# Normalising the first block by subtract and multiply, and forming its first weights' low parts on GpSimd

## Chip, cores and metric

The kernel runs on one core of one Trainium2 chip. The metric is the device time of one execution in microseconds (us). Each time stands for one execution of the whole program.

## The reference

The kernel computes one transformer-like block on an input of 2048 rows and 448 columns, all in 32-bit floats. Cut to what matters:

```python
mod = (silu(c) @ w_mod).reshape(1, 6, 1, 448)
sa, ca, ga, sb, cb, gb = (mod[:, i] for i in range(6))
h = layernorm(x) * (1 + ca) + sa
x = x + ga * A(h, k, v, ...)      # short causal convolution, times v, long causal convolution, times h
h = layernorm(x) * (1 + cb) + sb
g, u = h @ w_gate, h @ w_up       # 448 x 1792 each
x = x + gb * ((sigmoid(g) * u) @ w_down)
```

The change lies at the seam of the two halves: the second layer norm of the first 512 rows, and the first products of `h` with `w_gate` and `w_up`.

## The kernel before

**Tiles.** The 2048 rows stand as 16 tiles of 128 rows in one tensor `x1`. Four tiles make a block of 512 rows. The first half (convolutions by a fast transform, the gate) is followed by the gated feed-forward part, which runs over pairs (a slice `q` of 256 columns of the weights, a pair of row blocks `n`).

**Precision.** Every product of the feed-forward part is made of three products in a reduced format (`fp32r`): a number is kept as a high part (a copy rounded to `fp32r`, made by an ACT copy) and a low part (the number less its high part, a subtraction with two inputs). `plain_hi` (L553) and `plain_lo` (L557) do this for a slice of weights of 128 x 512, `x_hi` and `x_lo` (L697, L702 to L705) for the rows. High times high, low times high and high times low are added up in PSUM.

**Order of the work.** Nothing is reordered: each engine works through its own queue in the order in which the program names the operations. In the first half that order is the string `ORDER`, written out by hand. An item names a function and its arguments. Those that matter here, all near the end of the string:

- `gb.0` (L383): GpSimd adds a gated part to rows of `x1`.
- `fh` (`first_forms`): starts a weight load and makes the high parts of four weight tiles of the first slice on ACT (L553).
- `gm.0.3` (L487, L488), `ga.3` and `ga.2` (L421): GpSimd instructions, each of 128 x 896 with two inputs. Their results are first needed far later, at the gate of the second and third tile groups of the left half.
- `st`, `gma`, `gaa`, `bs`, `bt` (L349, L399, L404, L407 to L411): DVE's last work of the first half, which ends in the mean and variance `mv` of the four tiles of block 0.
- `y` (L364): products on TensorE that give the output of the long convolution. After the string follow two more groups of them, for `y1[1]` and `y1[2]`.

**The opening** of the second half comes next, in this order:

1. `ln2_end(0, 0)`: ACT takes the square root (L506), DVE the reciprocal `rstd2` (L508) and, by an operation of 128 x 4 with two inputs, `nmr2` = -mean * `rstd2` (L509).
2. `norm_rows(0)`: the rows are normalised as `x1 * rstd2 + nmr2` into `xn`, rows 0 to 2 on DVE (L666), row 3 on ACT (L668). Columns 128 to 191 are wanted twice side by side, in `xd`; four ACT activations make that straight from `x1` (L841). Between the two ACT copies `y1[1]` (`y_copy`, L372).
3. TensorE turns `xn` in 128 x 128 pieces (`turn_one`, L848). The 448 columns are cut into four tiles t = 0 to 3; tile 1 reads `xd`, the others `xn`. Tiles 0 and 2 come first, a row at a time (rows 0, 3, 1, 2), then 3, then 1.
4. Scale and shift by `cols`: DVE makes the high parts of tiles 0 and 2 from PSUM (`norm_hi`, L844), ACT those of tiles 3 and 1 (`norm_full`, L691). Then ACT copies `y1[2]` and makes the full values of tiles 0, 1 and 3, and DVE the four low parts of the weights (L557).
5. `plain_half(0, 0, 0, 0)`: 22 products of TensorE (L894) for the first 128 columns, eleven steps of two, in the order `LATE`. A step (t, s, b, k) takes weight tile t, s = 0 high and s = 1 low, and the rows' form b (0 is `B11`, 1 is `B21`) at place k. Places 0 and 1 of a form are high parts, the others low parts; place 1 of `B11` holds a high part in its upper 64 partitions and a low part in its lower 64. After the 8th product `last_vector` makes the full value of tile 2 on ACT and the three subtractions that give the rows' low parts on DVE (L702, L703, L705). After the 16th product `last_block` puts 16 products of `y` (L364, for `y1[3]`) into TensorE's queue and the gate and normalisation of block 1 into those of DVE (L935, L383, L500, L557, L666) and ACT.

The load of the next raw weights (`load_gu(1, ...)`) waits on SyncE's queue until the low parts are made, since it overwrites the raw weights.

Of the kernel before, what the change touches and what calls it, by code (L numbers as in the profile page):

```python
# [12 lines left out]
AF = mybir.ActivationFunctionType  # L13
OP = mybir.AluOpType
# [3 lines left out]
P = 128  # L18
# [29 lines left out]
gn.0.3 s2v.1.2:2 le.2 tv.1.5 kx.1.4:0 sa.1.1:1 yc.1 tv.1.3 gn.0.2 gn.1.2 sa.1.0:3 tv.1.6 st.1.1 gm.1.3 sum.3 st.1.0 s2v.1.3:1 sc.3 m0.1.2:0 y.0.0:0  # L48
m1.1.2:2 m0.1.3:3 kx.1.5:1 sa.1.2:2 ga.1 yc.0 m1.1.3:1 s2v.1.4:0 st.1.2 ga.0 kx.1.6:2 sa.1.3:1 m0.1.4:0 m1.1.4:2 gm.1.2 part.5:2 st.1.3 s2v.1.5:3
kx.1.7:0 pc.5 sa.1.4:0 m0.1.5:3 m1.1.5:1 s2v.1.6:1 st.1.4 gb.1 sa.1.5:3 m0.1.6:0 s2v.1.7:0 gm.0.2 m1.1.6:2 sum.5 st.1.5 sa.1.6:1 sc.5 m0.1.7:3  # L50
m1.1.7:1 y10.0:2 gb.0 st.1.6 fh sa.1.7:0 gma.0 gaa.0 gm.0.3 y.0.3:1 st.1.7 bs.1 y10.1:0 yc.3 bs.3 bs.2 y.0.2:2 gma.1 gaa.1 bt.3 bt.2 ga.3 bt.1 yc.2
bs.0 bt.0 ga.2
"""

# [58 lines left out]
def adaln_conv_glu_kernel(ctx: ExitStack, tc: tile.TileContext, q, kT, v, ssm, consts, dskip,  # L113
                          wgu, wd, wmod, c1t, wbt, out):
    nc = tc.nc
    PE, ACT, DVE, POOL = nc.tensor, nc.scalar, nc.vector, nc.gpsimd
# [51 lines left out]
    x1 = px.tile([P, NG, D], F32, name="x1")  # L168
# [28 lines left out]
    eps = cols[:, 20:21]  # L197
# [7 lines left out]
    rstd2, nmr2 = rstd, nmr  # L205
    mv = small([P, NG, nc.vector.BN_AGGR_DIM], "mv")
# [163 lines left out]
    def y_copy(h, i, y):  # L370
        t = copy_home((i - 1) % 2 if h else i)
        ACT.activation(t, y, AF.Copy)  # L372
        return t
# [129 lines left out]
    def ln2_end(i0, n_act=2):  # L503
        for i, j, w in ((i0, i0 + n_act, 1.0 / D), (i0 + n_act, i0 + 4, 1.0)):
            if i < j:
                ACT.activation(rstd2[:, i:j], mv[:, i:j, 1], AF.Sqrt, bias=eps, scale=w)  # L506
        s = slice(i0, i0 + 4)
        DVE.reciprocal(rstd2[:, s], rstd2[:, s])  # L508
        DVE.scalar_tensor_tensor(nmr2[:, s], mv[:, s, 0], -1.0, rstd2[:, s], op0=OP.mult, op1=OP.mult)  # L509
# [45 lines left out]
    def plain_lo(q, t, eng=DVE):  # L555
        x = plain(q, t)
        eng.tensor_sub(x[:, 1], ring["raw"][:, t], x[:, 0])  # L557
# [27 lines left out]
        for t in (2, 0, 1, 3):  # L585
            plain_hi(0, t)

    DO["fh"] = first_forms
    homes = {}

    def run(order):
# [40 lines left out]
    late["g02"], late["g03"] = copy_home(2), copy_home(3)  # L632
    yc = []
    y1 = [None, stage_out(1, 1, "t")]
    ln2_end(0, 0)
    y1.append(stage_out(1, 2, "t"))
    pz_.close()
    pa_.close()
# [5 lines left out]
    xn = xs[:, :4 * D].rearrange("p (a c) -> p a c", c=D)  # L644
    xd = xs[:, 4 * D:].rearrange("p (a c) -> p a c", c=P)
    ts = xs[:, :2048].rearrange("p (k t c) -> p k t c", k=2, t=2)
    full = pn.tile([P, 9, 512], F32, name="full")
# [9 lines left out]
    st = [st_t[:, 2 * k:2 * k + 2] for k in range(3)]  # L657
    xf = {"B11": a0[:, 0:3], "B21": a0[:, 3:7], "B22": a0[:, 7:11], "B12": a0[:, 11:14]}
# [3 lines left out]
    def norm_rows(n, rows_=range(4)):  # L662
        for i in rows_:
            g = slice(4 * n + i, 4 * n + i + 1)
            if n == 0 and i < 3 or n == 1 and i % 2:
                DVE.tensor_scalar(xn[:, i], x1[:, 4 * n + i], rstd2[:, g], nmr2[:, g], op0=OP.mult, op1=OP.add)  # L666
            else:
                ACT.activation(xn[:, i], x1[:, 4 * n + i], AF.Identity, bias=nmr2[:, g], scale=rstd2[:, g])  # L668

    def dup(eng):  # L670
        o, x = xd.rearrange("p a (r c) -> p a r c", r=2), xn[:, :, P:P + 64].unsqueeze(2).to_broadcast([P, 4, 2, 64])
        if eng is ACT:
            ACT.activation(o, x, AF.Copy)
        else:
            eng.tensor_copy(o, x)
# [13 lines left out]
    def norm_full(n, t, y, out=None):  # L689
        o = full[:, 4 * (n % 2) + t] if out is None else out  # L690
        ACT.activation(o, y, AF.Identity, bias=cols[:, 5 + t:6 + t], scale=cols[:, t:t + 1])  # L691
        if out is None and n % 2 and t == 3:
            for r in (0, 64):
                nc.sync.dma_start(full[r:r + 64, 8], full[0:64, 7])
# [4 lines left out]
    def x_lo(name, eng=DVE):  # L699
        o, x = xf[name], x_src[name]  # L700
        if o.shape[1] == 3:
            eng.tensor_sub(o[64:128, 1], x[64:128, 1], o[64:128, 1])  # L702
            eng.tensor_sub(o[:, 2], x[:, 0], o[:, 0])  # L703
        else:
            eng.tensor_sub(o[:, 2:4], x, o[:, 0:2])  # L705
# [128 lines left out]
        for t in ts_:  # L834
            plain_lo(q, t)

    norm_rows(0)
    yc.append(y_copy(1, 1, y1[1]))
    for i in range(4):
        x = x1[:, i, P:P + 64].unsqueeze(1).to_broadcast([P, 2, 64])  # L840
        ACT.activation(xd[:, i].rearrange("p (r c) -> p r c", r=2), x, AF.Identity, bias=nmr2[:, i:i + 1], scale=rstd2[:, i:i + 1])  # L841

    def norm_hi(t, y, out):
        DVE.tensor_scalar(out, y, cols[:, t:t + 1], cols[:, 5 + t:6 + t], op0=OP.mult, op1=OP.add)  # L844

    def turn_one(t, pt, i):
        at, w = AT[t]
        PE.transpose(pt[:, i * P:(i + 1) * P], xn[:, i, at:at + w] if w == P else xd[:, i], ident)  # L848

    p02 = two("y", "pt_02")  # L850
    p0, p2 = p02[:, 0], p02[:, 1]
    p13 = two("t", "pt_13")
    for i in (0, 3, 1, 2):
        turn_one(0, p0, i)
        turn_one(2, p2, i)
    for t in (3, 1):
        for i in range(4):
            turn_one(t, p13[:, t // 2], i)
# [1 line left out]
    norm_hi(2, p2, xf["B21"][:, 0])  # L860
    norm_full(0, 3, p13[:, 1], xf["B21"][:, 1])
    norm_full(0, 1, p13[:, 0], xf["B11"][:, 1])
    yc.append(y_copy(1, 2, y1[2]))
    norm_full(0, 0, p0)
    norm_full(0, 1, p13[:, 0])
    norm_full(0, 3, p13[:, 1])
    plain_lo(0, 2)
    plain_lo(0, 0)
    plain_lo(0, 1)
    load_gu(1, 0, 2)  # L870
    plain_lo(0, 3)
    load_gu(1, 2, 4)
    load_wd(1, wdraw)

# [7 lines left out]

    OPS = ((2, 0, 0, 0), (2, 1, 0, 0), (3, 0, 0, 1), (3, 1, 0, 1), (2, 0, 0, 2), (0, 0, 1, 0), (0, 1, 1, 0), (0, 0, 1, 2), (1, 0, 1, 1), (1, 1, 1, 1), (1, 0, 1, 3))
    OPS1 = tuple(x for x in OPS if x[0] < 2) + tuple(x for x in OPS if x[0] > 1)
    LATE = ((2, 0, 0, 0), (2, 1, 0, 0), (0, 0, 1, 0), (0, 1, 1, 0), (1, 0, 1, 1), (1, 1, 1, 1), (3, 0, 0, 1), (3, 1, 0, 1), (2, 0, 0, 2), (0, 0, 1, 2), (1, 0, 1, 3))

    def plain_half(p, q, n, f, between=None):
        xs_ = (("B11", "B21"), ("B12", "B22"))[n]
        pt = two("t" if p or f else "sa", f"gu{q}_{n}_{f}")
        ops = [(m, g) for m in range(11) for g in range(2)] if p in (0, 1, 2) and f == 0 else [(m, g) for g in range(2) for m in range(11)]  # L890
        order = LATE if p == f == 0 else OPS1 if p == 1 and f == 0 else OPS
        for i, (m, g) in enumerate(ops):
            t, s, b, k = order[m]
            PE.matmul(pt[:, g], plain(q, t)[:, s, g, f * P:f * P + P], xf[xs_[b]][:, k], start=m == 0, stop=m == 10, skip_group_check=True)  # L894
            if i == 7 and p == f == 0:
                last_vector()
            if i == (10 if p or f else 15) and between:
                between()
        sg = st[p % 2 * 2][:, f]
        ACT.activation(sg, pt[:, 0], AF.Sigmoid)  # L900
        mids.get((p, f), int)()
        DVE.tensor_mul(sg, sg, pt[:, 1])
        if p == f == 0:
            dup(DVE)
        finish_h(SL[p % 2][f], sg)
# [17 lines left out]
    SL = ((1, 2), (0, 3))  # L923
    act_stats = lambda *k: ln2_stats(*k, act=k)
    do = lambda f, *k, **w: lambda: f(*k, **w)
    def last_vector():
        norm_full(0, 2, p2)
        x_lo("B11")
        x_lo("B21")

    mids = {(0, 0): lambda: norm_rows(1, (0, 2)), (0, 1): lambda: split_wd_hi(0, 0)}

    def last_block():
# [316 lines left out]
```

## Time and profile before

| | |
|---|---|
| Median of 3 runs | 542.81 us |
| Lowest and highest | 542.04 and 543.7 us |
| Profiled execution, its own time | 542.78 us |
| Its span, first to last instruction | 541.0 us |
| TensorE clock granted, mean | 1.0 of full |
| TensorE (PE) busy | 528.5 us, 98% of the span |
| VectorE (DVE) busy | 437.7 us, 81% |
| ScalarE (ACT) busy | 272.7 us, 50% |
| GpSimd (POOL) busy | 56.4 us, 10%, its last instruction ends at 134.3 us |

The span starts at the first instruction. The profiled execution took 1.8 us more than its span, and it lies 0.03 us below the median. In a row of the timeline the columns are start, duration (of the whole group where several are merged), engine, line, operation, output and inputs, shape, count, and in brackets how long the engine had been idle and what ended it. Successive instructions of one engine overlap by some tens of ns, so the distance of two starts is a little less than a duration. A busy TensorE is not TensorE at its peak. A wait is put down to the releaser that came last by the profile.

### The profile page before, as it was taken

Reading aid. Unit: us, or ns where it says so; the run is one execution under the profiler, and the core shown is the slowest. Engines: PE = TensorE matmul, PEld = TensorE weight load, DVE = VectorE, ACT = ScalarE, POOL = GpSimd, SP = SyncE. Lnnn points to the kernel's source line nnn. Section 1 sums busy time; section 2 is a strip of 40 time slices with the busy share of each in tenths; the row PEclk is TensorE's granted clock in tenths of the full one; section 3 lists DMA queues with packets and bytes.
Section 4 is the critical chain, followed back from the end, with each engine's and each line's share of the span. In section 5 each row is a group of like instructions: output and inputs, shape, how many; then the busy total and the mean of one; then the engine's idle time right before and its main releaser. Section 6 shows DMA issues by size and latency. Waiting matters only on the chain.

```text
span 541.0 us, 7734 instructions
## 1 busy us (share of the span) xinstructions
PE 528.5 (98%) x2948; PEld 415.1 (77%) x2948; DVE 437.7 (81%) x548; ACT 272.7 (50%) x467; POOL 56.4 (10%) x48
## 2 busy tenths in 40 slices
PE   7999999898899999999999999999999999999997
PEld 7857622335688888888888888888888888888886
DVE  4799999999898878989988898875656466969565
ACT  6999999614775873675464434331212122424120
POOL 0000019999000000000000000000000000000000
PEclk9999999999999999999999999999999999999999
DMA  8996689850304074958883676675646660311003
GB/s 294 399 411 247 170 247 264 256 136 1 113 1 156 15 266 182 357 210 289 325 297 124 247 264 201 239 239 195 187 149 188 218 227 10 122 63 35 34 1 136
DMA packets 28198, 101.67 MB, mean 188 GB/s; under 512 B 3841, under 2 KB 4354, under 8 KB 27138
## 3 DMA queue, kind: packets, MB, share of 16 engines
q1 hardware_dynamic: 21826, 76.12, 42.8%
q10 hardware_dynamic: 6336, 25.06, 11.8%
q8 instruction: 23, 0.38, 0.3%
q14 instruction: 13, 0.11, 0.1%
HBM read 64.86 MB, written 28.44 MB: 172 GB/s over the span
## 4 chain that ended last, share of the span: by engine, by line
PE 83%; DVE 8%; ACT 3%; DMA 3%; issue 2%; SPq 0%; DVEq 0%; ACTq 0%
PE d L802 25%; PE b L768 17%; PE c L768 11%; PE a L768 11%; PE gu L894 5%; PE sa L345 3%; PE s1k L260 2%; PE kv L313 2%; PE s2v L332 2%; PE s2k L280 1%; PE s1v L260 1%; DMA zc<-in_c1t_dram 1%; DVE m L335 1%; DVE av L349 1%; PE pt L686 1%
## 5 line engine op out<-in xcount | busy, mean ns | idle before, releaser
L802 PE MATMUL d<-wd,h 128*128 128x448 f32 x666 | 144.5, 366 | 0.4 <-DVE wd L537 0.3
L802 PEld LDWEIGHTS d<-wd,h 128*128 128x128 f32 x666 | 124.7, 188 | 13.4 <-DVE wd L537 1.1
L768 PE MATMUL b<-xt,ring 128*128 128x512 f32 x408 | 99.1, 391 | 0.0
L768 PEld LDWEIGHTS b<-xt,ring 128*128 128x128 f32 x408 | 76.5, 188 | 14.9 <-issue 0.2
L817 DVE TENSOR_TENSOR x<-x,d 128x896 f32<-128x896 f32 x55 | 59.6, 1084 | 16.7 <-PE d L802 16.7
L768 PE MATMUL a<-x,ring 128*128 128x512 f32 x264 | 63.8, 389 | 0.0
L768 PEld LDWEIGHTS a<-x,ring 128*128 128x128 f32 x264 | 49.6, 188 | 10.3
L777 ACT ACTIVATE h<-st 128x512 fp32r<-128x512 f32 x55 | 34.6, 629 | 31.4 <-DVE st L786 19.0
L780 DVE TENSOR_TENSOR h<-st,h 128x512 fp32r<-128x512 f32 x55 | 37.8, 688 | 12.5 <-ACT h L777 12.2
L783 ACT ACTIVATE st<-st 128x512 f32<-128x512 f32 x24 | 15.2, 632 | 63.5 <-DVE st L1130 35.8
L894 PE MATMUL gu<-x,ring 128*128 128x512 f32 x176 | 42.6, 394 | 1.4 <-DVE x L702 1.3
L1084 ACT ACTIVATE st<-st 128x512 f32<-128x512 f32 x12 | 7.6, 631 | 68.1 <-DVE st L1083 68.1
L894 PEld LDWEIGHTS gu<-x,ring 128*128 128x128 f32 x176 | 32.6, 188 | 9.0 <-DVE x L702 1.8
L768 PE MATMUL c<-x,ring 128*128 128x512 f32 x144 | 34.8, 391 | 0.0
L749 ACT ACTIVATE ring<-sum 128x512 fp32r<-128x512 f32 x28 | 17.2, 626 | 32.2 <-DVE sum L730 16.9
L768 PEld LDWEIGHTS c<-x,ring 128*128 128x128 f32 x144 | 27.0, 188 | 5.4
L768 PE MATMUL c<-xt,ring 128*128 128x512 f32 x120 | 29.2, 389 | 0.0
L345 PE MATMUL sa<-m,const 128*64 128x448 f32 x128 | 27.3, 549 | 0.1
L786 DVE TENSOR_TENSOR st<-st 128x512 f32<-128x512 f32 x24 | 16.6, 690 | 11.9 <-ACT st L783 11.7
L768 PEld LDWEIGHTS c<-xt,ring 128*128 128x128 f32 x120 | 22.5, 188 | 4.6
L345 PEld LDWEIGHTS sa<-m,const 128*64 128x64 f32 x128 | 8.1, 136 | 16.9 <-issue 13.8
L1061 DVE TENSOR_TENSOR st<-b,st 128x1024 f32<-128x1024 f32 x11 | 13.5, 1223 | 9.1 <-PE b L768 8.9
(198 smaller groups left out, 823.0 us busy)
## 6 DMA issues: line engine op xcount, KB each, us to landing
fd<-ring ACTq DMA_DIRECT2D x35, 512.0 KB, 4.8
ring<-fd SPq DMA_DIRECT2D x35, 512.0 KB, 3.8
kTb<-ak SPq DMA_DIRECT2D x64, 112.0 KB, 3.9
wdk<-wd ACTq DMA_DIRECT2D x7, 896.0 KB, 5.2
wd<-wdk SPq DMA_DIRECT2D x7, 896.0 KB, 4.6
inb<-in_wgu_dram SPq DMA_DIRECT2D x6, 1024.0 KB, 5.4
kTa<-in_wmod_dram SPq DMA_DIRECT2D x12, 448.0 KB, 5.1
x<-in_q_dram SPq DMA_DIRECT2D x4, 896.0 KB, 10.8
```

The costliest lines, as they stand in the source:

```text
L260: PE.matmul(y, zc[r, g + jj], xs_[r, jj], start=True, stop=True)
L345: PE.matmul(wide[r, b, :, :56], wa[:, b, r], pairs2(ms[:, k])[:, b], start=True, stop=True)
L749: ACT.activation(forms[name, i][:, 0], w_src(name), AF.Copy)
L768: PE.matmul(pt, wh(s, t), x[:, k], start=start and m == 0, stop=stop and m == len(ops) - 1, skip_group_check=True)
L777: ACT.activation(hh, h, AF.Copy)
L780: DVE.tensor_sub(hl, h, hh)
L783: ACT.activation(y[:, 0], y[:, 0], AF.Sigmoid)
L786: DVE.tensor_mul(y[:, 0], y[:, 0], y[:, 1])
L802: PE.matmul(y, h[:, (2 * e + i) * P:(2 * e + i + 1) * P], x, start=m == 0, stop=m == len(ops) - 1)
L817: DVE.tensor_add(y, y, rows(pt))
L894: PE.matmul(pt[:, g], plain(q, t)[:, s, g, f * P:f * P + P], xf[xs_[b]][:, k], start=m == 0, stop=m == 10, skip_group_check=True)
L1061: DVE.tensor_add(u2, pb_, c1)
```

## The change

Five things are changed at the opening:

- `fl` follows `fh` in `ORDER`: the low parts of the first four weight tiles are made on GpSimd, ahead of `gm.0.3`, `ga.3` and `ga.2`, and no longer on DVE after the normalisation.
- `nmr2` of block 0 is not computed. DVE normalises all four rows with one operation each, `(x1 - mean) * rstd2`.
- `xd` is copied from `xn` by one ACT operation (`dup`), after the rows.
- Rows are turned in the order 0 to 3. DVE also makes the full value of tile 0 from PSUM; the low parts of the rows are four subtractions, each of one tile, named before the products and not inside them; ACT's copy of `y1[2]` moves behind the three full values that ACT still makes.
- In `LATE` the high-by-low step of tile 2 moves ahead of those with tile 3, and the last two steps change places.

```diff
-m1.1.7:1 y10.0:2 gb.0 st.1.6 fh sa.1.7:0 gma.0 gaa.0 gm.0.3 y.0.3:1 ...
+m1.1.7:1 y10.0:2 gb.0 st.1.6 fh fl sa.1.7:0 gma.0 gaa.0 gm.0.3 y.0.3:1 ...
...
-    DO["fh"] = first_forms
+    def first_low():
+        for t in (2, 0, 1, 3):
+            plain_lo(0, t, POOL)
+
+    DO["fh"], DO["fl"] = first_forms, first_low
...
-    ln2_end(0, 0)
+    ACT.activation(rstd2[:, 0:4], mv[:, 0:4, 1], AF.Sqrt, bias=eps, scale=1.0)
+    DVE.reciprocal(rstd2[:, 0:4], rstd2[:, 0:4])
     y1.append(stage_out(1, 2, "t"))
...
-    norm_rows(0)
     yc.append(y_copy(1, 1, y1[1]))
     for i in range(4):
-        x = x1[:, i, P:P + 64].unsqueeze(1).to_broadcast([P, 2, 64])
-        ACT.activation(xd[:, i].rearrange("p (r c) -> p r c", r=2), x, AF.Identity, bias=nmr2[:, i:i + 1], scale=rstd2[:, i:i + 1])
+        DVE.tensor_scalar(xn[:, i], x1[:, i], mv[:, i, 0:1], rstd2[:, i:i + 1], op0=OP.subtract, op1=OP.mult)
...
-    for i in (0, 3, 1, 2):
+    for i in range(4):
         turn_one(0, p0, i)
         turn_one(2, p2, i)
+    dup(ACT)
     for t in (3, 1):
...
-    yc.append(y_copy(1, 2, y1[2]))
-    norm_full(0, 0, p0)
+    norm_hi(0, p0, full[:, 0])
+    DVE.tensor_sub(xf["B11"][:, 2], full[:, 0], xf["B11"][:, 0])
     norm_full(0, 1, p13[:, 0])
     norm_full(0, 3, p13[:, 1])
-    plain_lo(0, 2)
-    plain_lo(0, 0)
-    plain_lo(0, 1)
+    norm_full(0, 2, p2)
+    DVE.tensor_sub(xf["B11"][64:128, 1], full[64:128, 1], xf["B11"][64:128, 1])
+    DVE.tensor_sub(xf["B21"][:, 3], full[:, 3], xf["B21"][:, 1])
+    DVE.tensor_sub(xf["B21"][:, 2], full[:, 2], xf["B21"][:, 0])
+    yc.append(y_copy(1, 2, y1[2]))
     load_gu(1, 0, 2)
-    plain_lo(0, 3)
     load_gu(1, 2, 4)
...
-    LATE = (... (3, 0, 0, 1), (3, 1, 0, 1), (2, 0, 0, 2), (0, 0, 1, 2), (1, 0, 1, 3))
+    LATE = (... (2, 0, 0, 2), (3, 0, 0, 1), (3, 1, 0, 1), (1, 0, 1, 3), (0, 0, 1, 2))
...
-            if i == 7 and p == f == 0:
-                last_vector()
...
-    def last_vector():
-        norm_full(0, 2, p2)
-        x_lo("B11")
-        x_lo("B21")
```

The functions that it calls, unchanged:

```python
def plain_lo(q, t, eng=DVE):
    x = plain(q, t)
    eng.tensor_sub(x[:, 1], ring["raw"][:, t], x[:, 0])

def dup(eng):
    o, x = xd.rearrange("p a (r c) -> p a r c", r=2), xn[:, :, P:P + 64].unsqueeze(2).to_broadcast([P, 4, 2, 64])
    if eng is ACT:
        ACT.activation(o, x, AF.Copy)
```

More of the change, by code (lines that the diff above doesn't have):

```diff
@@ L50 @@
 kx.1.7:0 pc.5 sa.1.4:0 m0.1.5:3 m1.1.5:1 s2v.1.6:1 st.1.4 gb.1 sa.1.5:3 m0.1.6:0 s2v.1.7:0 gm.0.2 m1.1.6:2 sum.5 st.1.5 sa.1.6:1 sc.5 m0.1.7:3
-m1.1.7:1 y10.0:2 gb.0 st.1.6 fh sa.1.7:0 gma.0 gaa.0 gm.0.3 y.0.3:1 st.1.7 bs.1 y10.1:0 yc.3 bs.3 bs.2 y.0.2:2 gma.1 gaa.1 bt.3 bt.2 ga.3 bt.1 yc.2
+m1.1.7:1 y10.0:2 gb.0 st.1.6 fh fl sa.1.7:0 gma.0 gaa.0 gm.0.3 y.0.3:1 st.1.7 bs.1 y10.1:0 yc.3 bs.3 bs.2 y.0.2:2 gma.1 gaa.1 bt.3 bt.2 ga.3 bt.1 yc.2
 bs.0 bt.0 ga.2
@@ L884, in adaln_conv_glu_kernel @@
     OPS1 = tuple(x for x in OPS if x[0] < 2) + tuple(x for x in OPS if x[0] > 1)
-    LATE = ((2, 0, 0, 0), (2, 1, 0, 0), (0, 0, 1, 0), (0, 1, 1, 0), (1, 0, 1, 1), (1, 1, 1, 1), (3, 0, 0, 1), (3, 1, 0, 1), (2, 0, 0, 2), (0, 0, 1, 2), (1, 0, 1, 3))
+    LATE = ((2, 0, 0, 0), (2, 1, 0, 0), (0, 0, 1, 0), (0, 1, 1, 0), (1, 0, 1, 1), (1, 1, 1, 1), (2, 0, 0, 2), (3, 0, 0, 1), (3, 1, 0, 1), (1, 0, 1, 3), (0, 0, 1, 2))
     def plain_half(p, q, n, f, between=None):
```

## The prediction

> **What bounds the kernel now.** I read the page first, then the busy time by stage, TensorE's timeline around the change, and the chain.
>
> ```profile
> span 541.0 us, 7734 instructions
> ```
> ```profile
> 133.50:158.30 24.80, 21.53 (x108) 15.85 (x108) 21.50 (x37) 20.41 (x35) 0.79 (x1) 1.00 0.19 61
> 158.30:541.00 382.70, 379.33 (x1763) 326.67 (x1763) 293.94 (x359) 149.14 (x246) 0.00 (x0) 1.00 0.50 176
> ```
>
> The columns are stretch, length, busy time of PE, its weight loads, DVE, ACT and POOL, clock and DMA. From 158.3 on TensorE is busy for 379.33 of 382.70 us: what the opening wins or loses is carried to the end. Only 133.5 to 158.3 can move, and there TensorE stands idle for 3.3 us.
>
> ```profile
> 129.80 3.67 PE L364 MATMUL y<-av,spare 128*64 128x224 f32 x34
> 134.96 2.95 PE L848 MATMUL pt<-ident,xn 128*128 128x128 f32 x16 [1.48 <-POOL tmp L421]
> 137.66 3.32 PE L894 MATMUL gu<-x,ring 128*128 128x512 f32 x12
> 142.31 1.19 PE L894 MATMUL gu<-x,ring 128*128 128x512 f32 x4 [1.33 <-DVE x L702]
> 143.43 1.80 PE L364 MATMUL y<-av,spare 128*64 128x224 f32 x16
> 145.16 1.67 PE L894 MATMUL gu<-x,ring 128*128 128x512 f32 x6
> ...
> 158.28 1.89 PE L802 MATMUL d<-wd,h 128*128 128x448 f32 x8 [0.32 <-DVE wd L537]
> ```
>
> TensorE waits 1.48 us for the normalised rows and 1.33 us for the rows' low parts, and 0.32 us at 158.28 for DVE. The chain says that DVE, not TensorE, leads in between:
>
> ```profile
> 144.13 1.01 DVE inb L935
> ...
> 157.23 1.01 DVE wd L537
> ```
>
> So two clocks are to be forecast: the start of L935 on DVE (144.05) and the end of the first 22 products (145.16 and six more). With 22 products in 5.00 us,
>
> ```profile
> 169.15 5.00 PE gu L894 x22
> ```
>
> one is 0.227 us and that end is 146.5. As TensorE has 0.32 us to spare at 158.28, the shift of the end is the later of DVE's shift and TensorE's less 0.3.
>
> **What goes.** DVE's and ACT's opening today:
>
> ```profile
> 132.31 0.18 DVE L508 RECIPROCAL rstd<-rstd 128x4 f32<-128x4 f32 x1 [0.43 <-ACT rstd L506]
> 132.52 1.79 DVE L509 SCALAR_TENSOR_TENSOR nmr<-mv,rstd 128x4 f32<-128x4 f32 x1
> 134.34 1.36 DVE L666 TENSOR_SCALAR xn<-x,rstd,nmr 128x448 f32<-128x448 f32 x3
> 136.24 1.53 DVE L844 TENSOR_SCALAR x<-pt,cols 128x512 fp32r<-128x512 f32 x2 [0.53 <-PE pt L848]
> 137.68 2.49 DVE L557 TENSOR_TENSOR ring<-tmp,ring 128x512 fp32r<-128x512 f32 x4
> 141.57 0.69 DVE L702 TENSOR_TENSOR x<-full,x 64x512 fp32r<-64x512 f32 x1 [1.40 <-ACT full L691]
> ```
> ```profile
> 144.05 1.08 DVE L935 TENSOR_TENSOR inb<-inb,tmp 128x896 f32<-128x896 f32 x1
> ```
> ```profile
> 135.89 1.64 ACT L841 ACTIVATE xn<-x,nmr,rstd 128x128 f32<-128x128 f32 x4
> 137.95 1.45 ACT L691 ACTIVATE x<-pt,cols 128x512 fp32r<-128x512 f32 x2 [0.42 <-PE pt L848]
> 139.28 0.92 ACT L372 ACTIVATE tmp<-y 128x896 f32<-128x896 f32 x1
> 140.08 2.12 ACT L691 ACTIVATE full<-pt,cols 128x512 f32<-128x512 f32 x3
> ```
>
> L509 goes (1.79 us, on the path), L557 goes from DVE (2.49 us; beside ACT's work, but products wait for it), L841 goes from ACT (1.64 us), and ACT's copy of 0.92 us at 139.28 no longer stands between the rows' forms. The SyncE loads that waited for L557 are issued earlier; nothing is queued behind them that waits, and their first reader comes after L935's successors, so I cost them at nothing.
>
> **What L509 waited for.** It handles four elements a partition, and at 151.11, with GpSimd done, it takes 0.16 us. Its like, L474, was stretched in the same way:
>
> ```profile
> 130.13 4.15 POOL L421 TENSOR_TENSOR tmp<-tmp,zc 128x896 f32<-128x896 f32 x2
> ```
> ```profile
> 96.30 2.08 POOL L487 TENSOR_TENSOR kTa<-kTa,arow 128x896 f32<-128x896 f32 x1
> ```
> ```profile
> 96.96 1.45 DVE L474 TENSOR_TENSOR nmr<-nmr,rstd 128x4 f32<-128x4 f32 x1
> ```
> ```profile
> 151.11 0.16 DVE L509 SCALAR_TENSOR_TENSOR nmr<-mv,rstd 128x4 f32<-128x4 f32 x1
> ```
>
> L421 ends at 134.28 and L509 at 134.31; L487 ends at 98.38 and L474 at 98.41. A DVE operation with two inputs in SBUF is held until the running GpSimd instruction ends. L508, with one input, is not held (0.18 us in the midst of L421).
>
> **What is added on GpSimd.** Four instructions of 128 x 512 come ahead of three that today fill the time from 125.78:
>
> ```profile
> 123.71 2.11 POOL L383 TENSOR_TENSOR x<-x,kTa 128x896 f32<-128x896 f32 x1
> ...
> 125.78 2.10 POOL L487 TENSOR_TENSOR zc<-zc,arow 128x896 f32<-128x896 f32 x1
> 127.96 2.10 POOL L488 TENSOR_TENSOR zc<-zc,brow 128x896 f32<-128x896 f32 x1
> ```
>
> By elements one is 2.10 * 512 / 896 = 1.20 us. Four are 4.8 us: GpSimd's queue ends at 134.28 + 4.8, about 139.1, and L487 runs from 130.6 to 132.7. The high parts that they read are there (ACT makes them in parallel, the next row). No GpSimd row writes `fp32r`; on DVE that costs nothing (L557 0.62 us each), so I take 1.20, with 2.40 as the far end.
>
> ```profile
> 123.17 2.19 ACT L553 ACTIVATE ring<-tmp 128x512 fp32r<-128x512 f32 x4 [0.52 <-DVE m L335]
> ```
>
> The low parts are there at 130.6, ahead of every product that reads them, and the three that are pushed back (to 139.1) feed nothing in the opening; the cost is in whom GpSimd holds.
>
> **The four normalisations.** They are ready to go at 132.52, where L509 stood. Undisturbed, starts lie (1.36 - 0.51) / 2 = 0.43 us apart, with one of 0.51:
>
> ```profile
> 134.34 0.51 DVE L666 TENSOR_SCALAR xn<-x,rstd,nmr 128x448 f32<-128x448 f32 x1
> ```
>
> Are they held as L509 was? They have one tensor input, and 448 elements in 0.43 us are 1.04 per ns, while the subtractions of two inputs run 512 in (2.49 - 0.68) / 3 = 0.60 us, 0.85 per ns, and the statistics of one input run slower still, while GpSimd works:
>
> ```profile
> 127.76 1.46 DVE L407 BATCH_NORM_STATS2 st<-x 128x6 f32<-128x392 f32 x3
> ```
>
> So the bounds are: not held (as L407 and L508), or held (as L509). An operation faster than one element per step of L407 must fetch by more than one path, and the second path is what two-input operations use; I take held. The Trainium skill, page "SBUF — State Buffer", section "Who interferes with whom", says it outright: a `tensor_scalar` in a two-port mode and a GpSimd instruction exclude each other, each for its whole length. By that rule the time is 544.6 us, by the nearest one-input rows 540.1; no row of this trace shows the case.
>
> The second choice is who goes next when both wait. GpSimd's next instruction is due 0.08 us after its last one (125.78 + 2.10 to 127.96), while a normalisation holds the path for some 0.4 us; so GpSimd waits before the second normalisation has been issued. I take turn and turn about, the first to ask going first. The one row of a GpSimd instruction that met a two-input DVE operation shows that GpSimd got in between two of these; whether the second came late for that, or for a wait of its own, the rows do not tell:
>
> ```profile
> 21.19 0.75 DVE L305 SCALAR_TENSOR_TENSOR m<-kTa,const,m 112x512 f32<-112x512 f32 x1
> 22.05 0.96 DVE L305 SCALAR_TENSOR_TENSOR kTa<-kTa,const,spare 112x512 f32<-112x512 f32 x1
> ```
> ```profile
> 21.75 0.70 POOL L229 TENSOR_TENSOR inb<-inb,gbrow 1x224 f32<-1x224 f32 x1 [15.92 <-DMA inb<-in_ssm_dram]
> ```
>
> **The sum.** First normalisation 132.7 (L487 ends) to 133.1; L488 to 135.2; second to 135.6; first L421 to 137.7; third to 138.1; second L421 to 140.2; fourth to 140.7. Today DVE's three rows are done at 134.34 + 1.36 = 135.7. Then two transposes (16 in 2.95, some 0.4 with the tail) to 141.1, and DVE's high parts (two in 1.53) at 141.9 and 142.6. ACT's one copy `dup` of 512 elements (L553: 0.55 to 0.62) runs from 140.7 to 141.3, while TensorE turns tile 3, then tile 1, to 141.9. Products start at 141.9 (today 137.66). ACT's five forms at 0.69 each (2.12 / 3 and less) end at 142.4, 143.1, 143.8, 144.5 and 145.2. DVE: full value of tile 0 to 143.4, and the subtractions at 0.6 each follow to 145.8, the last bound by ACT. No product waits for them in the new order: the 16 products run to 145.5, the 16 of L364 (143.43 to 145.16, 1.73) to 147.3, the last six to 148.6, against 146.5: 2.1 later, of which 0.3 is spare. L935 starts at 145.8 against 144.05: 1.8 later. All behind it is unchanged. The profiled execution's 542.78 (1.8 beyond its span, and 0.03 under the median) becomes **544.6 us**. Its own range, with the order of turns and the GpSimd price moving the last normalisation by a us either way, is 543.6 to 545.6.
>
> **Rivals.**
>
> 1. VectorE keeps the path (the other side). Once the first normalisation has it at 132.7, the other three follow without GpSimd getting in: rows done at 134.5, high parts from 134.9, full value of tile 0 at 137.2. L488 runs 134.5 to 136.6, the first L421 to 138.7; the subtractions, two inputs each, are held till then and run to 141.1. L935 is 2.9 earlier: 539.9 us. For it: operations of DVE overlap (0.51 long, 0.43 apart). Against it: GpSimd has asked before. It decides if the fourth normalisation ends before 140.7 - 1.8 = 138.9.
> 2. Normalisations are not held at all. Rows done at 134.3; but the subtractions, due at 137.0, are held as L509 was until GpSimd ends at 139.0, and end at 141.4: L935 2.65 earlier, 540.1 us. For it L407 and L508, against it the rate of L666.
> 3. Two normalisations pass at each gap: rows done at 136.6, the subtractions wait for GpSimd's end at 140.7 and end at 143.2; 0.85 earlier, 541.9 us.
> 4. GpSimd needs 2.40 us for an `fp32r` output. With turns, the fourth normalisation ends at 141.3, and GpSimd's last instruction, at 145.4, holds the subtractions: L935 at about 147.8, 546.6 us.
> 5. The clock falls. In the forecast TensorE does only six transposes between 133.5 and 140.7. The granted clock is 1.00 in both stretches above, whose longest wait is 1.48 us. At half clock for eight products there are 8 * 0.227 = 1.8 us more: 546.4 us. The Trainium skill, page "TensorE: Matmul & The Clock Gate", section on the clock gate, puts the window at about 3.4 us, within which an idle TensorE is set to half clock; here each gap is some 2.2 us.
>
> **How the numbers follow.** Forecast 0.45, rival 1 0.22, rival 2 0.15, rivals 3, 4 and 5 0.06 each. About 0.3% (1.6 us) is what a measurement of this kernel can tell from no change: faster means under 541.2, slower over 544.4. Faster: rivals 1 and 2, 0.37. Within: rival 3 and a third of the forecast, 0.21. Slower: 0.42. The range takes in the forecast and rivals 1 to 3, from 539.4 (half a us under rival 1) to 545.8; rivals 4 and 5 are left out.
>
> **What would show it.** In the profile after: no L509 before 150; four operations of 128 x 448 on DVE from 132.5, with durations of some 2 us against 0.51 and GpSimd instructions ending where they end; the last ending near 140.7. GpSimd's four of 128 x 512 at 1.20 from 125.8, its queue ending near 140.2. L935 near 145.8, the products starting near 141.9 and without a wait inside. It is wrong if the normalisations last 0.5 us each and lie together (rivals 1 and 2; then a subtraction is held near 138), or if TensorE shows a wait past 158 that is not there now.

## The result and the profile after

| | before | after |
|---|---|---|
| Median | 543.7 us (9 runs, 542.04 to 545.02) | 546.49 us (9 runs, 544.97 to 548.03) |
| Ratio of the times, 95% interval | | 1.0057 [1.004, 1.0074] |
| Profiled execution | 542.78 us, span 541.0 | 548.03 us, span 546.2 |
| Mean TensorE clock granted, profiled execution | 1.0 | 0.987 |

The change makes the kernel slower by 0.57%, about 3.1 us (0.0057 * 543.7). The forecast was 1.8 us slower, and the median lies above its range. About half of the distance between 544.6 and 546.49 us is not the change: the forecast stood on an execution of 542.78 us at full clock, and the median of the kernel before is 543.7 us over nine runs.

The first view is the page of the changed kernel: its span, and the granted clock in 40 slices of 13.7 us each.

```profile
span 546.2 us, 7732 instructions
...
PEclk9999999799799999999999999999999999999999
```

The two digits 7 stand for 95.6 to 109.2 us and for 136.6 to 150.2 us; the page of before has only nines. The first one lies ahead of everything that the change touches. This profiled execution met a fall of the clock there which the execution profiled before did not meet, and which executions of both kernels meet (runs e9 and e13, below). It makes the changed trace late by a constant when the opening begins, as the same DVE instruction shows, which started at 127.76 before:

```profile
129.93 1.46 DVE L407 BATCH_NORM_STATS2 st<-x 128x6 f32<-128x392 f32 x3
...
134.69 7.12 DVE L844 TENSOR_SCALAR xn<-x,mv,rstd 128x448 f32<-128x448 f32 x4
...
148.39 1.08 DVE L933 TENSOR_TENSOR inb<-inb,tmp 128x896 f32<-128x896 f32 x1
```

129.93 less 127.76 is 2.17 us. All times of this trace are to be read less 2.17 where they are compared with before or with the forecast; 548.03 less 542.78 less 2.17 leaves 3.08 us for the change, near the 3.1 us of the ratio. (The medians differ by 2.79 us; both hold executions with and without that fall.) L933 is the line that was L935: 148.39 less 2.17 is 146.22, against 144.05 before.

The four normalisations take 7.12 us where three took 1.36. GpSimd's and TensorE's timelines say what they waited for and what it does to TensorE:

```profile
127.95 5.01 POOL L557 TENSOR_TENSOR ring<-tmp,ring 128x512 fp32r<-128x512 f32 x4
132.91 2.10 POOL L487 TENSOR_TENSOR zc<-zc,arow 128x896 f32<-128x896 f32 x1
135.09 2.10 POOL L488 TENSOR_TENSOR zc<-zc,brow 128x896 f32<-128x896 f32 x1
137.27 4.28 POOL L421 TENSOR_TENSOR tmp<-tmp,zc 128x896 f32<-128x896 f32 x2
```
```profile
135.57 0.44 PE L851 MATMUL pt<-ident,xn 128*128 128x128 f32 x2
137.50 0.44 PE L851 MATMUL pt<-ident,xn 128*128 128x128 f32 x2 [1.48 <-DVE xn L844]
139.68 0.44 PE L851 MATMUL pt<-ident,xn 128*128 128x128 f32 x2 [1.74 <-DVE xn L844]
141.86 2.39 PE L851 MATMUL pt<-ident,xn 128*128 128x128 f32 x10 [1.74 <-DVE xn L844]
143.91 5.26 PE L899 MATMUL gu<-x,ring 128*128 128x512 f32 x16
149.10 1.80 PE L364 MATMUL y<-av,spare 128*64 128x224 f32 x16
...
163.23 2.07 PE L807 MATMUL d<-wd,h 128*128 128x448 f32 x8
```

One normalisation passes at each end of a GpSimd instruction: the transposes that follow each of them start at 137.50, 139.68 and 141.86, 2.18 us apart like GpSimd's starts at 132.91, 135.09 and 137.27. The first is hardly delayed, since L487 ends soon after it starts (135.01); the other three are held for a whole GpSimd instruction each. And the 16 products take 5.26 us, 0.33 each, where 22 took 5.00. The table by stage, with the clock in the column behind POOL, says why:

```profile
139.00:141.00 2.00, 0.44 (x2) 0.20 (x2) 2.00 (x2) 0.00 (x0) 2.00 (x2) 0.75 0.00 0
141.00:143.00 2.00, 1.14 (x6) 1.14 (x7) 1.22 (x2) 0.63 (x1) 0.55 (x1) 0.50 0.00 0
143.00:145.00 2.00, 2.00 (x9) 1.81 (x8) 1.97 (x4) 0.71 (x2) 0.00 (x0) 0.50 0.03 8
145.00:147.00 2.00, 2.00 (x7) 1.58 (x6) 1.12 (x2) 2.00 (x5) 0.00 (x0) 0.54 0.00 0
147.00:150.00 3.00, 3.00 (x20) 2.12 (x20) 2.93 (x5) 1.56 (x3) 0.00 (x0) 1.00 0.00 0
```

A mean of 0.75 over 2 us is half clock for the last 1.0 us, 0.54 is half clock for the first 1.84: the clock is at half from 140.0 to 146.84, 6.84 us, right when the rows are there and TensorE has work without a gap. The shift at the end has the size of TensorE's own: L364 starts at 149.10 less 2.17 = 146.93, 3.50 later than before (143.43). TensorE's wait of 0.32 us at 158.28 is gone (163.23 has none), so that some 3.2 of it reach the end; DVE's L933 is only 2.17 later, and TensorE leads.

### The profile page after: what moved, and what is told of

Its sections match the earlier page's. It is cut to its first block, busy times and chain, and to the rows that moved or that the text cites. A ratio compares the mean times of both kernels' runs of the same rounds, so it can differ in the third digit from the quotient of the medians.

```text
span 546.2 us, 7732 instructions
## 1 busy us (share of the span) xinstructions
PE 532.6 (98%) x2948; PEld 418.6 (77%) x2948; DVE 440.6 (81%) x546; ACT 270.4 (50%) x462; POOL 62.5 (11%) x52
## 4 chain that ended last, share of the span: by engine, by line
PE 93%; DVE 3%; DMA 2%; issue 1%; ACT 1%; ACTq 0%
PE d L807 25%; PE b L773 17%; PE c L773 11%; PE a L773 11%; PE gu L899 8%; PE sa L345 4%; PE s2v L332 3%; PE s2k L280 3%; PE s1k L260 2%; PE kv L313 2%; PE s1v L260 2%; DVE xn L844 1%; PE y L364 1%; DMA zc<-in_c1t_dram 1%; PE part L433 1%; PE pt L691 1%
## 5 line engine op out<-in xcount | busy, mean ns | idle before, releaser
L899 PEld LDWEIGHTS gu<-x,ring 128*128 128x128 f32 x176 | 33.8, 194 | 7.2 <-issue 0.3
```

## The experiments

My theory after the first look had two parts: the normalisations are held once for each GpSimd instruction, which the low parts have moved into their way; and TensorE, given 0.44 us of work in each 2.18 us, loses its clock for the products that follow. The rivals were that only one of the two counts, or that the loss comes from another part of the change (the normalisation by subtract and multiply, the new order). Ratios below are to the kernel before on the same chip, whose medians were 543.62 to 544.16 us.

**e1: GpSimd's late instructions away.**

```diff
-... gma.0 gaa.0 gm.0.3 y.0.3:1 ... bt.3 bt.2 ga.3 bt.1 yc.2
-bs.0 bt.0 ga.2
+... gma.0 gaa.0 y.0.3:1 ... bt.3 bt.2 bt.1 yc.2
+bs.0 bt.0
```

> The changed kernel without the four GpSimd instructions of 128x896 that follow the low parts (the last gate products gm.0.3, ga.3 and ga.2 are left out, so two gated parts of the result are missing). Theory, holding: the four normalisations take 0.5 us each and end at 134.4 on the clock of the kernel before, no subtraction is held, the granted clock stays at 1.0 between 130 and 160, and the kernel is 3.5 to 4.5 us faster than the kernel before. Rival, the new order itself is at fault (ACT's one copy after the rows, four separate subtractions): the opening stays late whatever GpSimd does, and the kernel is slower than the kernel before or the same.

Measured: 539.99 us, 0.9923 [0.9903, 0.9943]. The normalisations on DVE and TensorE's products:

```profile
134.05 1.78 DVE L844 TENSOR_SCALAR xn<-x,mv,rstd 128x448 f32<-128x448 f32 x4
```
```profile
134.93 2.35 PE L851 MATMUL pt<-ident,xn 128*128 128x128 f32 x16
137.23 3.92 PE L899 MATMUL gu<-x,ring 128*128 128x512 f32 x16
```

With GpSimd idle from 132.31 the four run in 1.78 us, 0.42 apart, the transposes follow in one piece, and the products go at 3.92 instead of 5.26 us. It is GpSimd's work that holds the normalisations: with nothing on GpSimd to meet them the changed kernel is 4.2 us faster than the kernel before.

**e4: the kernel before, with only the low parts moved to GpSimd.**

```diff
-... gb.0 st.1.6 fh sa.1.7:0 ...
+... gb.0 st.1.6 fh fl sa.1.7:0 ...
-    plain_lo(0, 2)
-    plain_lo(0, 0)
-    plain_lo(0, 1)
     load_gu(1, 0, 2)
-    plain_lo(0, 3)
```

> The kernel before with nothing changed but the first weights' low parts, which GpSimd makes behind fh. Theory, holding: L509 is held only until L487 ends, then each of the three normalisations on VectorE is held for about 2.2 us, the rows are done near 139.4, the clock falls to half for some us, and the kernel is 2.5 to 4.5 us slower than the kernel before: one part alone does the harm. Rival, the move to GpSimd is harmless and takes 2.5 us off VectorE: 1 to 2 us faster.

Measured: 548.3 us, 1.0085 [1.0066, 1.0104], 4.6 us slower, a little more than expected. DVE and the stages:

```profile
134.87 6.72 DVE L670 TENSOR_SCALAR xn<-x,rstd,nmr 128x448 f32<-128x448 f32 x3
```
```profile
137.00:139.00 2.00, 0.63 (x4) 0.42 (x4) 2.00 (x2) 1.05 (x3) 1.95 (x1) 0.82 0.01 4
139.00:141.00 2.00, 0.69 (x2) 0.29 (x2) 2.00 (x2) 0.00 (x0) 2.00 (x2) 0.50 0.00 0
```

The move of the low parts alone gives the whole loss and more: the old form of the normalisation (multiply and add) is held in the same way, 2.29 us each on average, and the clock is at half from 138.3 on. So the rival that the loss comes from subtract and multiply, or from the new order, falls: by the two ratios the other parts of the change win back some 1.5 us, though their intervals just overlap (from 1.0066 here, to 1.0074 there).

**e3: the changed kernel, low parts back on VectorE behind the high parts.**

```diff
-... gb.0 st.1.6 fh fl sa.1.7:0 ...
+... gb.0 st.1.6 fh sa.1.7:0 ...
...
+    for t in (2, 0, 1, 3):
+        plain_lo(0, t)
```

> The changed kernel with the first weights' low parts on VectorE again, after the two high parts of the rows; all else as changed. Theory, holding: GpSimd's queue ends 5 us earlier, the first normalisation is held for about 1.8 us (as L509 was) and the other three take 0.5 us each, the clock stays at 1.0, and the kernel is within 1 us of the kernel before, on the fast side. Rival, the subtract-and-multiply normalisation and the new order cost the time: 2 us or more slower than the kernel before.

Measured: 543.49 us, 0.9993 [0.9977, 1.0008]. The four normalisations and GpSimd's last instructions:

```profile
133.62 3.31 DVE L844 TENSOR_SCALAR xn<-x,mv,rstd 128x448 f32<-128x448 f32 x4
```
```profile
131.27 4.14 POOL L421 TENSOR_TENSOR tmp<-tmp,zc 128x896 f32<-128x896 f32 x2
```

Only the first is held, to GpSimd's end at 135.41; the loss is gone, and no gain is left: the hold of the first (3.31 against 1.78 us in e1) is nearly as long as the wait of L509 (1.79 us in the prediction) that the change removes.

**e2 and e5: products that nobody reads, in TensorE's gaps.** 12 and 6 of them behind the transposes of rows 0 to 2; nothing else is changed.

```diff
         turn_one(0, p0, i)
         turn_one(2, p2, i)
+        for _ in range(6 if i < 3 else 0):
+            PE.matmul(p13[:, 0, :P], ones, ones, start=True, stop=True)
```

> The changed kernel with 12 products of ones after each of the first three rows' transposes, written into PSUM that is overwritten later, so that TensorE is not idle while it waits. Theory, holding and then the clock: the normalisations are held as before the edit (2.26 us each), the granted clock stays at 1.0, the 16 products and the transposes before them take 2.5 us less than the 7.3 us from the fourth normalisation to the first product of L364, and about 2 us of the 3.1 us that the change costs are gone: 0.5 to 1.3 us slower than the kernel before. Rival, the fall of the clock costs nothing because VectorE is behind anyway: no change against the changed kernel, about 3 us slower than the kernel before.

> As the run with 12 products of ones after each of the first three rows' transposes, but with six of them: there a group took 2.84 us, more than the wait of 1.74 us that it was to fill, and held the transposes up by itself. Theory, holding and then the clock: the normalisations are held as in the changed kernel (last one ending about 7.1 us after the first has begun), the clock stays at 1.0 between 130 and 150, from the fourth normalisation to the first product of L364 it takes about 4.8 us in place of 7.3, and the kernel is 0.5 to 1.3 us slower than the kernel before. Rival, VectorE is behind anyway: about 3 us slower, as the changed kernel.

Measured: 547.28 us with 12, 1.0054 [1.0035, 1.0073]; 545.04 us with 6, 1.0028 [1.0013, 1.0043]. TensorE with 12, and then DVE, TensorE and the stages with 6:

```profile
138.89 2.84 PE L860 MATMUL pt<-ones 128*128 128x128 f32 x24
141.57 1.25 PE L851 MATMUL pt<-ident,xn 128*128 128x128 f32 x10
```
```profile
133.98 7.16 DVE L844 TENSOR_SCALAR xn<-x,mv,rstd 128x448 f32<-128x448 f32 x4
```
```profile
139.28 1.50 PE L860 MATMUL pt<-ones 128*128 128x128 f32 x12
141.20 1.40 PE L851 MATMUL pt<-ident,xn 128*128 128x128 f32 x10 [0.41 <-DVE xn L844]
142.54 3.93 PE L901 MATMUL gu<-x,ring 128*128 128x512 f32 x16
146.40 1.80 PE L364 MATMUL y<-av,spare 128*64 128x224 f32 x16
```
```profile
139.00:141.00 2.00, 1.78 (x14) 1.59 (x14) 2.00 (x1) 0.00 (x0) 1.89 (x1) 1.00 0.00 0
141.00:143.00 2.00, 1.80 (x12) 1.48 (x13) 1.47 (x3) 0.99 (x2) 0.00 (x0) 1.00 0.00 0
```

Twelve took 2.84 us, longer than the gap of 1.74, so that the products themselves kept the transposes waiting (in the trace with 12 the normalisations were done 2.4 us before the last transposes): that run says nothing by its time. Six fit. The normalisations are held as before (they take 7.16 us), the clock stays at 1.00, and from the last transposes to L364 it is 146.40 - 141.20 = 5.20 us; in the changed kernel it is 149.10 - 141.86 = 7.24. The clock's part at this place is 2.04 us. By the times, holding costs 1.5 us with the clock kept up (by the interval 0.7 to 2.3), and about the other half of the 3.1 us goes with the clock; 1.5 is slightly more than the 0.5 to 1.3 expected. In its profiled execution L407 starts at 129.22, 1.46 later than in that of before, and 545.43 less 542.78 less 1.46 leaves 1.19 us.

**e6: one SBUF input.** If the hold is about VectorE's second path to SBUF, an operation that reads one SBUF tensor only and does not take two elements at a time must pass. The reciprocal goes to PSUM, and a row is (x1 - mean) times that.

```diff
-    DVE.reciprocal(rstd2[:, 0:4], rstd2[:, 0:4])
+    rp = two("sa", "rp")[:, 0, 0:4]
+    DVE.reciprocal(rp, rstd2[:, 0:4])
...
-        DVE.tensor_scalar(xn[:, i], x1[:, i], mv[:, i, 0:1], rstd2[:, i:i + 1], op0=OP.subtract, op1=OP.mult)
+        DVE.scalar_tensor_tensor(xn[:, i], x1[:, i], mv[:, i, 0:1], rp[:, i:i + 1].to_broadcast([P, D]), op0=OP.subtract, op1=OP.mult)
```

> The changed kernel with the reciprocal written to PSUM and each normalisation made by an operation that reads x1 from SBUF and the reciprocal from PSUM: one input in SBUF, and one element at a time. Theory (what is held is a second path into SBUF, used by two inputs or by two elements at a time): the four take about 0.7 us each although GpSimd works through the whole of them, and end at 135.2 on the clock of the kernel before; the first subtraction is held until GpSimd ends near 139.1; the clock stays at 1.0; 2 to 3 us faster than the kernel before. Rival (GpSimd holds any VectorE operation that streams this much from SBUF): they are held for 2 us each, as in the changed kernel, and about 3 us slower than the kernel before.

Measured: 541.86 us, 0.9969 [0.9955, 0.9982], faster than both kernels; 1.7 us by the ratio, a little less than the 2 to 3 expected. GpSimd and DVE:

```profile
132.91 2.09 POOL L487 TENSOR_TENSOR zc<-zc,arow 128x896 f32<-128x896 f32 x1
135.07 2.09 POOL L488 TENSOR_TENSOR zc<-zc,brow 128x896 f32<-128x896 f32 x1
137.24 4.18 POOL L421 TENSOR_TENSOR tmp<-tmp,zc 128x896 f32<-128x896 f32 x2
```
```profile
134.67 2.46 DVE L845 SCALAR_TENSOR_TENSOR xn<-x,mv,rp 128x448 f32<-128x448 f32 x4
...
139.94 2.04 DVE L869 TENSOR_TENSOR x<-full,x 128x512 fp32r<-128x512 f32 x1
```

The four run back to back in 2.46 us, to 137.13, through the end of L487 and nearly the whole of L488; the subtraction L869, with two SBUF inputs, is held until 141.42, where GpSimd ends, to the end at 141.98. The Trainium skill, page "SBUF — State Buffer", section "Who interferes with whom", states both halves: a VectorE instruction with at most one SBUF input, outside the two-port modes, does not contend with GpSimd, and one with two SBUF inputs does; the two rows agree with both.

**e7 and e11: fewer low parts on GpSimd, on top of e6.** e7 leaves tiles 1 and 3 there, and VectorE makes tile 2 ahead of the rows' high parts and tile 0 behind them; e11 leaves tiles 2, 0 and 1, and VectorE makes tile 3 ahead of the subtraction for place 3 of `B21`.

```diff
-        for t in (2, 0, 1, 3):
+        for t in (1, 3):
...
+    plain_lo(0, 2)
     norm_hi(0, p0, xf["B11"][:, 0])
     norm_hi(2, p2, xf["B21"][:, 0])
+    plain_lo(0, 0)
```
```diff
-        for t in (2, 0, 1, 3):
+        for t in (2, 0, 1):
...
+    plain_lo(0, 3)
     DVE.tensor_sub(xf["B21"][:, 3], full[:, 3], xf["B21"][:, 1])
```

> The run before this one, with the low parts of weight tiles 1 and 3 on GpSimd and those of tiles 2 and 0 on VectorE, around the rows' high parts: GpSimd ends 2.5 us earlier, near 136.6, before the first subtraction is due. Theory: no operation on VectorE is held, L935's counterpart starts near 141.0, 2.5 to 3.5 us faster than the kernel before. Rival: VectorE's 1.2 us more of work cancel it, no faster than the run before this one.

> The one-SBUF-input kernel with three low parts (tiles 2, 0 and 1) on GpSimd and the fourth (tile 3) on VectorE behind the opening, ahead of the subtraction of the first block's next place. GpSimd's run then ends some 1.25 us earlier, near 140.2 us, and the first subtraction behind the products of the opening (2.04 us, held, with four) takes near its unheld 0.7 to 1.0 us. Theory that this subtraction's hold is on the path: 0 to 1 us below the one-input kernel with four, ratio 0.995 to 0.997. Rival (the path runs over another engine by then, or the low part on VectorE costs its 0.9 us there): same as with four or up to 0.5 us slower.

Measured: e7 542.57 us, 0.9974 [0.9957, 0.9991]; e11 540.77 us, 0.9936 [0.9914, 0.9957]. GpSimd and DVE in e7, then DVE in e11:

```profile
133.66 4.14 POOL L421 TENSOR_TENSOR tmp<-tmp,zc 128x896 f32<-128x896 f32 x2
```
```profile
135.89 2.45 DVE L557 TENSOR_TENSOR ring<-tmp,ring 128x512 fp32r<-128x512 f32 x1
```
```profile
137.21 0.86 DVE L869 TENSOR_TENSOR x<-full,x 128x512 fp32r<-128x512 f32 x1
```

My expectation for e7 failed: VectorE's own low part has two SBUF inputs, so it took 2.45 us, waiting for L421 (to 137.80) in the place of the others, and e7 is no better than e6: its executions at clock 1.0 lie at 540.9 to 541.05 us, the one of e6 at 539.89. In e11 no two-input operation comes before GpSimd is nearly done, the first one is stretched to 0.86 instead of 2.04 us, and the median is 1.1 us under e6. About half of that is the edit: at clock 1.0 e11 stands at 539.33 and 539.35 us against 539.89, and with the fall near 100 us out of both (e12 and e10, below) the medians differ by 0.43. The rest goes with the clock, which was at 1.0 in 2 of 6 executions of e11 and in 1 of 12 of e6.

**e8, e9 and e10: the fall near 100 us.** Executions of the kernel before lie at 542.15 to 542.6 us with a mean clock of 0.999 or 1.0, at 543.6 to 544.3 with 0.996 or 0.997, and at 544.6 to 545.4 with 0.993 (17 runs beside e1). A stretch at half clock as long as that of 140.0 to 146.84 takes 6.84 / 2 / 541 = 0.0063 off the mean, and half of it 0.0032: the levels 0.997 and 0.993 to 0.994 are one and two stretches of 3.4 us (the traces of e1 and e3 to e7 show one each near 100 us, that of the changed kernel two). e8 put seven ones products into TensorE's queue (item `fz` of `ORDER`) where I took the wait to be, and landed late; e9 put six of them right ahead of the products of `y` that wait; e10 is e6 with the six. The first diff is that of e8 (seven products, into the third `part`), the second that of e9, e10, e12 and e13.

```diff
-... sc.3 m0.1.2:0 y.0.0:0
+... sc.3 m0.1.2:0 fz y.0.0:0
```
```diff
-... m1.1.0:2 m0.1.1:3 y.0.1:3 kx.1.3:2 ...
+... m1.1.0:2 m0.1.1:3 fz y.0.1:3 kx.1.3:2 ...
...
+    def keep_busy():
+        for _ in range(6):
+            PE.matmul(held_ps["part", (4,)][:, 0, :P], ones, ones, start=True, stop=True)
+
+    DO["fz"] = keep_busy
```

> The kernel before with nothing but seven products of ones in TensorE's wait near 98.6 (idle for 1.9 us), written to PSUM that is read no more. Theory (the spread of the kernel before, 542.2 at a mean clock of 1.0 to 545.4 at 0.993, is a fall of the clock near 100 in some executions, which comes of an idle stretch just before it): fewer or no executions with a clock under 1.0, the median 0.8 to 1.5 us lower. Rival: the fall has another cause, median and spread as they are.

> The kernel before with one thing added: six 128x128 products of the ones tile, whose result nobody reads, issued on TensorE right ahead of the y products whose wait of 1.9 to 2.1 us near 98.6 us goes before the half clock of 99 to 106 us in those executions that show it; the seven products of the kept-busy run before this landed behind that stretch. Theory (the granted clock falls where TensorE has done little for some microseconds, and this is what spreads the times of the kernel before): the products take some 1.2 us out of the wait, the clock stays at 1.0 in all or nearly all executions, and the median is 0.5 to 1.3 us below the kernel before, near the 542.2 to 542.6 us of its executions at clock 1.0. Rival (the fall there has another cause, or the products are not enough): the same share of executions at 0.993 to 0.997, no difference in time within 0.5 us.

> The one-SBUF-input kernel (reciprocal and mean-subtracted rows by one operation with its factor in PSUM) with the same six ones products ahead of the y products near 98.6 us. Theory: the two gains add, all executions at clock 1.0, some 2.5 us below the kernel before (ratio near 0.9955). Rival: the products change nothing, ratio as without them, 0.997.

Measured: e8 544.94 us, 1.0036 [1.002, 1.0051]; e9 542.41 us, 0.9971 [0.996, 0.9982]; e10 540.02 us, 0.9928 [0.9911, 0.9946]. TensorE near 100 us in the changed kernel's execution (which fell), in e8, and in e9:

```profile
99.94 3.25 PE L364 MATMUL y<-av,spare 128*64 128x224 f32 x16 [2.08 <-issue]
```
```profile
99.90 1.80 PE L364 MATMUL y<-av,spare 128*64 128x224 f32 x16 [1.76 <-issue]
...
107.70 1.83 PE L591 MATMUL part<-ones 128*128 128x128 f32 x14
```
```profile
97.52 0.98 PE L332 MATMUL s2v<-av,const 64*64 64x448 f32 x8
98.43 1.60 PE L591 MATMUL part<-ones 128*128 128x128 f32 x12
100.03 1.80 PE L364 MATMUL y<-av,spare 128*64 128x224 f32 x16
```

In e8 the wait of 1.76 us is still there and the products come some 9 us behind the place of the fall, so e8 says nothing about it; half of its 12 executions have 0.994 to 0.996, and they pay for the products. In e9 the wait is filled: all 12 executions have 0.999 or 1.0, against 4 of 17 of the kernel before beside them. The fall near 100 us does come from TensorE's wait there. e10 gains 4.1 us, more than the 2.5 expected; all 6 of its executions have 0.999 or 1.0, and only one of e6's 12 did, which stood at 539.89 us.

**e12 and e13: both gains together, and the changed kernel with the wait near 98.6 us filled.** e12 is e11, and e13 the changed kernel, each with the six products of e9.

> The one-SBUF-input kernel with three low parts on GpSimd, and the six ones products ahead of the y products near 98.6 us. Both gains were measured apart: 539.33 to 539.35 us in the executions of three low parts at clock 1.0, and no execution below clock 0.999 with the products. Theory: they add, all executions at clock 0.999 or 1.0, median 539.2 to 539.8 us, ratio near 0.9915. Rival (the products cost as much as they give where the rest is earlier): 540.5 us or more.

> The changed kernel with the six ones products ahead of the y products near 98.6 us, and nothing else; beside it stands the kernel before with the same products (542.41 us), so that the fall of the clock near 100 us is out of both. Theory (the loss comes from the opening alone: normalisations held, then some 6.8 us at half clock): median 3 to 3.5 us above the kernel before with the products, 545.4 to 545.9 us, executions at clock 0.990 to 0.995, half clock near 138 to 145 us only. Rival (part of the loss belongs to the fall near 100 us, which no execution of the changed kernel was free of): 544.5 us or less.

Measured: e12 539.59 us, 0.9922 [0.9905, 0.9938], the fastest of all; its executions have clock 0.999 or 1.0. e13 545.67 us, 1.0036 [1.0022, 1.0049]. The stages of e13:

```profile
99.00:101.00 2.00, 1.42 (x14) 1.20 (x15) 2.00 (x3) 1.07 (x4) 2.00 (x2) 1.00 1.03 408
...
139.00:141.00 2.00, 1.28 (x6) 1.28 (x7) 1.22 (x2) 0.63 (x1) 0.41 (x1) 0.50 0.00 0
141.00:143.00 2.00, 2.00 (x9) 1.81 (x8) 1.97 (x4) 0.85 (x2) 0.00 (x0) 0.50 0.00 0
143.00:145.00 2.00, 2.00 (x6) 1.52 (x6) 1.11 (x2) 2.00 (x4) 0.00 (x0) 0.50 0.00 0
```

With the fall near 100 us out of both kernels the change costs 545.67 - 542.41 = 3.26 us by the medians of e13 and e9, or 3.5 by their ratios (1.0036 / 0.9971 = 1.0065). So the loss belongs to the opening alone, and the rival that part of it lies near 100 us falls.

## Why the prediction was wrong

**Right: what bounds the kernel, and what is held.** From 158 us on nothing gave back what the opening lost, beyond the 0.3 us of spare. The choice "I take held" was right (e1 against the changed kernel: 1.78 and 7.12 us), and so was the forecast that one normalisation passes for each GpSimd instruction: rivals 1, 2 and 3, which would have ended near 540 to 542 us, did not happen. GpSimd's price for an `fp32r` output was right too: 1.25 us each by 5.01 for four, where 1.20 was taken, so rival 4 is out.

**Mis-sized, the other way: the turns.** The forecast let GpSimd's next instruction wait for the normalisation between, some 0.4 us each time, and put the last ending at 140.7. GpSimd did not wait: L488 starts 0.08 us behind L487's end (132.91 + 2.10 to 135.09), as it did without normalisations between; only the last one, the second L421, took 0.12 us longer (2.22 against 2.10). So by GpSimd's spans the hold runs one way here: that the two exclude each other, each for its whole length, holds for VectorE alone, and "turn and turn about" with both sides waiting was not what happened. The last normalisation ended at 141.81 less 2.17 = 139.64, 1.06 us earlier than put.

**Mis-sized: the way from there to L364 at full clock.** The forecast has 4.8 us (140.7 to 145.5), e5 5.3 (141.14 to 146.40): sixteen products took 3.93 and ten transposes 1.40. With the turns put right, this gives L364 at 139.64 + 5.26 = 144.90, 1.47 later than before, and some 1.2 at the end once the spare 0.3 is used; DVE gives the same, with L935 1.23 later in e5 (146.74 less 1.46). The products did start where they were put (143.91 less 2.17 = 141.74 against 141.9), but only because two misses cancel: the turns were over early, and the last ten transposes took 2.39 us at half clock instead of 1.40. At full clock the forecast's +1.8 would have come out as +1.2, on its side and in its range; e5 measured +1.5 by its ratio and +1.2 in its profiled execution.

**The step that failed: rival 5, "The clock falls".** It was set apart as a rival at 0.06 and left out of the range, and the forecast's own sum kept all products at full clock (the 16 products from 141.9 to 145.5, 3.6 us, where 5.26 were measured). The grounds were that the clock had stayed at 1.00 from 133.5 us on in the trace of before, with 1.48 us as the longest wait. But the forecast had itself worked out what counts, "TensorE does only six transposes between 133.5 and 140.7", and gaps in a row with little between them are another thing than one. In the changed kernel's opening no wait is longer than 1.74 us, and still the clock falls, behind the second gap: in the 3.4 us ahead of 140.0 TensorE did 0.44 us of transposes at 137.50 and 0.32 from 139.68 on, 0.76 in all. The half clock cost 2.04 us (7.24 against 5.20 from the last transposes to L364); the rival had priced it at 1.8. So the chance was wrong and the mechanism right; the price came near by other terms, since it counted eight products, 3.6 us at half clock, where the trace has 6.84 us with a wait of 1.74 us in it. That its 546.4 us lies 0.1 from the median is luck: its base was 0.9 us too low and its hold 0.6 too high. 1.2 us for the hold and 2.04 for the clock make 3.2 us, against the 3.1 measured.

The page named beside that rival, "TensorE: Matmul & The Clock Gate" of the Trainium skill, Part 1, says that the clock is halved after an idle window of about 3.4 us, and that these windows run freely. By the runs the lengths agree: 6.84 us at half is two of them, and the steps of the mean clock are multiples of one. Idle in the sense of no work at all was not needed: a window in which TensorE worked for 0.76 of 3.4 us was enough, while stretches with 1.78 of 2.00 us (e5) kept the clock up.

**Left open.** How little work lowers the clock is known only for this opening. In the 3.41 us ahead of the fall TensorE worked for 0.76 us in the changed kernel, 0.88 in e13 and 1.20 in e4; in e5, with 2.64 us from 138.65 to 142.06, there was no fall. Near 100 us the busy time alone does not tell:

```profile
95.63:99.04 3.41, 2.23 (x26) 1.26 (x22) 3.38 (x5) 3.31 (x12) 3.33 (x3) 1.00 0.88 237
136.59:140.00 3.41, 0.76 (x4) 0.41 (x4) 3.41 (x3) 0.00 (x0) 3.33 (x3) 1.00 0.08 31
```

Both rows are of the changed kernel and end where the clock falls, the first after 2.23 us of work; the execution of before worked for only 1.51 us in the 3.41 us up to 100.51, the end of its wait, and kept the full clock. No run separates what the many small products there (128 x 1) count for from where the wait lies in time. How long a fall lasts went with the work in its first 3.41 us: with 2.73 us or more it ended there (e1 and e3 to e7, near 100 us); with 1.67 (from 140.0) and 2.51 (from 99.04) in the changed kernel, and 0.72 and 2.44 in the openings of e4 and e13, it lasted another 3.41. Nor was it measured which of VectorE's and GpSimd's instructions holds the path for how long where one passes: the held normalisation ends 0.26 us behind the GpSimd instruction (141.81 and 141.55), while GpSimd's next starts 0.08 us behind it or at once.

## What to carry to other kernels

Before work is moved to GpSimd, list which VectorE operations will meet it: here those with two SBUF inputs waited for GpSimd's end, and so did the row scaling of one input that runs at 448 elements in 0.43 us; the four passed one at each end of a GpSimd instruction, and a form with one SBUF tensor and its factor in PSUM freed them (7.12 to 2.46 us). When a forecast leaves TensorE with several short gaps in a row, add up its work over 3 to 4 us; where that is near the 0.76 to 1.20 us at which the clock fell here, charge the next 7 us at half clock to the sum itself. A spread of the times that follows the mean clock is worth a look: six idle products in one wait of 2 us took it away, and 1.75 us off the median.

## What was not expected of the hardware

- The clock fell to half for 6.84 us after two gaps of only 1.48 and 1.74 us, with 0.44 us of work between them.
- A held VectorE operation costs GpSimd next to nothing: L487, L488 and L421 start 2.18 us apart with normalisations passing between them, as before without, and the two L421 together take 4.28 us against 4.15.
- Most of the kernel's spread before, 542.04 to 545.02 us, comes from one wait near 98.6 us whose effect on the clock differs from one execution to the next; with it filled, 12 executions lie between 542.07 and 543.1 us.
